# GpSimd's pooling sums of keys and values in pieces of at most 256 columns

## The chip, the cores and the metric

The kernel runs on one core of a Trainium2 chip. The metric is the device time of one execution in microseconds (us). TensorE is called PE in the profile (its weight loads PEld), VectorE is DVE, ScalarE is ACT, GpSimd is POOL, and SyncE, which only issues transfers here, is SP.

## The reference, cut to what matters

Attention with pooled keys and values, then two layers of experts:

```python
k_p = k.reshape(B, H, S // 8, 8, D).mean(axis=3)     # B, H, S, D = 8, 8, 576, 64
v_p = v.reshape(B, H, S // 8, 8, D).mean(axis=3)
scores = q @ k_p.T / sqrt(D);  attn = softmax(scores);  out = attn @ v_p
x = out as (4608, 512)
logits = cosine(x, expert_emb) / tau                 # 8 experts, top 1
x[rows of e] = gate * relu(x @ w1[e]) @ w2[e]        # for each expert e
out = max(x @ m1, x @ m2, x @ m3) @ mo               # (4608, 512)
```

The change concerns the means of eight neighbouring rows of `k` and `v`.

## The kernel before, in words

All of it is one program. The first 200 us are the attention stage: 36 tiles of 128 queries go through a software pipeline (`for it in range(NT + 4)`), in which PE computes scores (`psc`), transposes the weights (`paT`), transposes the next queries (`pqT`) and multiplies by the values (`pav`), in this order in each pass. DVE takes, for each tile, the row maxima (`mx`, L451), the differences (`sh`, L454), the reciprocal sums (`rs`, L500 and L502), the scaled output (`x`, L510) and the routing logits (`dt`, `lg`, L515 and L517). The tiles `psc` and `pav` have one buffer each: PE may overwrite `psc` when `sh` is done, and `pav` when `dt` is done. The two expert layers follow and keep PE busy to the end.

Each of the 8 batches b has its own preparation (`prep_steps`). Its keys lie in the tile `kraw` (`kt` in the code) as 5 chunks of rows, the first four with 128 rows, the last with 64; each row holds 8 neighbours of 64 columns. Its values lie in `vraw` (`vt`) in the same way. The sum over the neighbours is a tree in place, with widths w = 4, 2 and 1: add the upper half to the lower one. `pool_k2` (L262 to L269) does it for the keys of batches 2 to 7, `pool_v` (L275 to L282) for the values of all batches, both on POOL. For batches 0 and 1 DVE sums the keys (L257). After them `spread_v` (L284 to L293), also on POOL, writes the sums into the block layout `vbd` in five instructions. PE transposes the sums (`ptk`, `ptv`). Two generations of `kraw` and `vraw` exist, so the load of batch b + 2 waits on SP's queue until batch b is summed.

The order on every engine is the order of the program. The routing is put between the work of DVE by hand: `fill` takes small steps from a queue and puts them behind the instructions of a tile (`FILL`). Routing works in rounds over groups of tiles (`CHK`). The first round, `rank_steps(0)`, is queued after tile 8, the second, `rank_steps(1)`, after tile 17. A round begins with one scaling of the logits (`lg`, L551), a maximum, a difference (L547), a masked weight (`wt`, L556), a comparison (`oh`, L547), a copy (`pre`, L617) and four adds of a prefix sum (`pre`, L547). Earlier, a few constants are made in the same way (`tokid`, L1422; `im`, L551).

Waits on one engine's own results are semaphore waits too: an instruction that reads what an earlier one of the same engine wrote carries a wait for it, an instruction that reads something else carries none.

Of the kernel before, what the change touches and what calls it, by code (L numbers as in the profile page):

```python
# [14 lines left out]
A = mybir.AluOpType  # L15
# [6 lines left out]
def attention_moe_moe_kernel(  # L22
# [24 lines left out]
    nc = tc.nc  # L47
# [68 lines left out]
    if True:  # L116
# [61 lines left out]
        if True:  # L178
# [69 lines left out]
            def prep_steps(b):  # L248
                kt, vt = kv[b]
                kb, vb = kbds[b % 3], vbds[b % 3]  # L250
                kp = qp.tile([P, 5, 2, D], F32, tag="kp", name=f"kp{b}")
# [11 lines left out]
                def pool_k2():  # L263
                    for c0, c1, n in ((0, 4, P), (4, 5, RC[4])):
                        for w in (4, 2, 1):
                            dst = kt[0:n, c0:c1, 0:w, :] if w > 1 else kp[0:n, c0:c1, 0:1, :]
                            nc.gpsimd.tensor_tensor(
                                dst, kt[0:n, c0:c1, 0:w, :], kt[0:n, c0:c1, w : 2 * w, :], op=A.add
                            )  # L269

                def dup_k():
                    for c0, c1, n in ((0, 3, P), (3, 4, KC[3]), (4, 5, KC[4])):
# [1 line left out]

                def pool_v(c0, c1, n):  # L275
                    for w in (4, 2, 1):
                        for a0 in range(c0, c1, 2) if w == 4 else (c0,):
                            a1 = min(a0 + 2, c1) if w == 4 else c1
                            dst = vt[0:n, a0:a1, 0:w, :] if w > 1 else vp[0:n, a0:a1, :].unsqueeze(2)
                            nc.gpsimd.tensor_tensor(  # L280
                                dst, vt[0:n, a0:a1, 0:w, :], vt[0:n, a0:a1, w : 2 * w, :], op=A.add
                            )  # L282
# [77 lines left out]
                if b == 0:  # L360
                    return [
                        lambda: (pool_all(), dup_k(), trans_k(range(4), 0, 7), trans_k([4], 7, 8)),
                        lambda: (pool_v(0, 4, P), pool_v(4, 5, 64), spread_v()),
                        lambda: (trans_v(0, 4), trans_v(4, 5)),
                        lambda: vdot(),
                    ]
                if b == 1:
                    pk = [lambda c=c: pool_k(c) for c in range(5)]
                    pk += [lambda: (pool_v(0, 4, P), pool_v(4, 5, 64))]
                else:  # L370
                    return [
                        lambda: (pool_k2(), pool_v(0, 4, P), pool_v(4, 5, 64)),
                        spread_v,
                        lambda: trans_kv(range(4), 0),
                        lambda: trans_kv([4], 4 * P),
                        vdot,
                    ]
# [1425 lines left out]
```

## Time and profile before

| what | value |
| --- | --- |
| median of 3 runs | 1263.38 us (1262.02 to 1263.81) |
| the profiled execution's time | 1260.98 us |
| its span on the core | 1259.2 us |
| PE busy | 1215.6 us, 97% of the span |
| DVE busy | 799.2 us, 63% |
| POOL busy | 318.9 us, 25%, in 383 instructions |
| mean granted clock of PE | 0.991 of full speed |

Busy time is the time in which an engine had an instruction running, waits inside an instruction included. The profiled execution is 2.4 us faster than the median of the runs, and its span is 1.8 us shorter than its time.

### The profile page before, as it was taken

To read this page: it belongs to the slowest core of one execution; us is meant where nothing else is said; L and a number is where in the kernel's file an instruction comes from. 1 tells how busy PE (TensorE), PEld (TensorE's weight loads), DVE (VectorE), ACT (ScalarE), POOL (GpSimd) and SP (SyncE) were. 2 spreads that over 40 slices of the span, in tenths; PEclk is the share of its full clock that TensorE was granted. 3 is DMA by queue.
4 is the path that set the end of the run, shared out by engine and by line. 5 is a ranking of instruction groups with operands and counts; after the bars stand their busy time and mean duration, and the time that the engine had idled before them with its cause. 6 is when DMAs were issued, how large, how long until landed. Compare 5 with 4: busy or idle time off the path is not lost. (4 is left out here: it accounts for less than half of the span.)

```text
span 1259.2 us, 22318 instructions
## 1 busy us (share of the span) xinstructions
PE 1215.6 (97%) x8251; PEld 1158.0 (92%) x8251; DVE 799.2 (63%) x1575; ACT 580.5 (46%) x1040; POOL 318.9 (25%) x383
## 2 busy tenths in 40 slices
PE   5899899999999999999999999999999999999995
PEld 4788789999999999999999998998998998998994
DVE  6676886797889999898764446345445454454450
ACT  3466465545666676666655333323223323223221
POOL 6985553420212212222000302103103004004001
PEclk9899999999999999999999999999999999999998
DMA  9968246423976445844619666475564673773721
GB/s 252 267 202 236 97 138 217 151 85 32 298 262 226 164 143 203 283 151 137 207 51 350 241 238 242 160 262 205 207 239 182 220 264 153 258 263 124 253 108 52
DMA packets 98038, 246.21 MB, mean 196 GB/s; under 512 B 17100, under 2 KB 58106, under 8 KB 89858
## 3 DMA queue, kind: packets, MB, share of 16 engines
q1 hardware_dynamic: 84770, 189.09, 44.5%
q0 software_dynamic: 13152, 55.62, 13.3%
q8 instruction: 67, 1.10, 0.4%
q14 instruction: 49, 0.40, 0.1%
HBM read 252.23 MB, written 46.98 MB: 238 GB/s over the span
## 5 line engine op out<-in xcount | busy, mean ns | idle before, releaser
L1617 PE MATMUL p<-yhi,wt 128*128 128x384 f32 x1512 | 387.2, 336 | 0.0
L1617 PEld LDWEIGHTS p<-yhi,wt 128*128 128x128 f32 x1512 | 273.4, 188 | 0.6
L1617 PE MATMUL p<-ylo,wt 128*128 128x384 f32 x756 | 254.0, 336 | 0.0
L1625 ACT COPY s<-p 128x384 f32<-128x384 f32 x162 | 77.8, 480 | 221.1 <-PE p L1617 216.8
L1104 PE MATMUL py<-hhi,whi 128*128 128x256 f32 x576 | 164.6, 286 | 0.0
L1104 PE MATMUL py<-hhi,wlo 128*128 128x256 f32 x576 | 163.1, 283 | 1.6 <-DVE wlo L1036 1.6
L1056 PE MATMUL ph<-xhi,whi 128*128 128x256 f32 x576 | 163.8, 284 | 0.7 <-DVE hlo L1072 0.7
L1056 PE MATMUL ph<-xhi,wlo 128*128 128x256 f32 x576 | 163.0, 283 | 0.7 <-DVE wlo L1036 0.7
L1056 PE MATMUL ph<-xlo,whi 128*128 128x256 f32 x576 | 163.0, 283 | 0.0
L1104 PE MATMUL py<-hlo,whi 128*128 128x256 f32 x576 | 162.9, 283 | 0.0
L1617 PEld LDWEIGHTS p<-ylo,wt 128*128 128x128 f32 x756 | 142.1, 188 | 0.5
L1646 DVE TENSOR_TENSOR blk<-p,s 128x384 f32<-128x384 f32 x108 | 59.7, 553 | 113.9 <-PE p L1617 113.9
L1602 POOL DMA_INDIRECT gt<-gbuf,ix x26 | 37.0, 1424 | 312.1 <-DMA ix<-idbuf 305.7
L1104 PEld LDWEIGHTS py<-hhi,wlo 128*128 128x128 f32 x576 | 110.4, 192 | 1.8 <-DVE wlo L1036 1.8
L1056 PEld LDWEIGHTS ph<-xhi,whi 128*128 128x128 f32 x576 | 110.5, 192 | 1.2 <-DVE hlo L1072 0.9
L1056 PEld LDWEIGHTS ph<-xhi,wlo 128*128 128x128 f32 x576 | 110.5, 192 | 0.9 <-DVE wlo L1036 0.9
L1056 PEld LDWEIGHTS ph<-xlo,whi 128*128 128x128 f32 x576 | 110.5, 192 | 0.0
L1104 PEld LDWEIGHTS py<-hlo,whi 128*128 128x128 f32 x576 | 110.5, 192 | 0.0
L1104 PEld LDWEIGHTS py<-hhi,whi 128*128 128x128 f32 x576 | 110.4, 192 | 0.0
L1036 DVE TENSOR_TENSOR wlo<-w2raw,whi 128x1024 fp32r<-128x1024 f32 x84 | 102.2, 1221 | 8.8 <-ACT whi L1034 8.7
L1036 DVE TENSOR_TENSOR wlo<-w1raw,whi 128x1024 fp32r<-128x1024 f32 x67 | 81.8, 1220 | 27.6 <-ACT whi L1034 26.5
L1034 ACT CAST whi<-w2raw 128x1024 fp32r<-128x1024 f32 x88 | 91.8, 1044 | 7.7 <-PE py L1104 4.7
(316 smaller groups left out, 2280.8 us busy)
## 6 DMA issues: line engine op xcount, KB each, us to landing
wt<-wdram SPq DMA_DIRECT2D x51, 1792.0 KB
w1raw<-in_moe_w_dram SPq DMA_DIRECT2D x88, 512.0 KB
w2raw<-in_moe_w_dram SPq DMA_DIRECT2D x88, 512.0 KB
wdram<-wst POOLq DMA_DIRECT2D x9, 1792.0 KB
ybuf<-yo SPq DMA_DIRECT2D x40, 256.0 KB
cvraw<-in_moe_w_dram POOLq DMA_DIRECT2D x36, 256.0 KB
vraw<-in_v_dram SPq DMA_DIRECT2D x8, 1024.0 KB
xbuf<-x SPq DMA_DIRECT2D x16, 512.0 KB
```

Source lines behind the costliest of these rows:

```text
L1034: nc.scalar.copy(hi, src)
L1036: eng.tensor_tensor(lo, src, hi.bitcast(F32), op=A.subtract)
L1056: nc.tensor.matmul(ps[:, f, :], a_[:, c, fs], b_[:, c, :], start=(n == 0), stop=(n == 3 * DC - 1))
L1104: nc.tensor.matmul(py[:, c // 2, (c % 2) * 256 : (c % 2 + 1) * 256], a_[:, f, c * P : (c + 1) * P], b_[:, f, :], start=(piece == 0 and f = ...
L1602: nc.gpsimd.indirect_dma_start(out=gt[g][:, j : j + 1], out_offset=None, in_=gbuf[:, :], in_offset=bass.IndirectOffsetOnAxis(ap=cols[j], a ...
L1617: nc.tensor.matmul(ps, a_, b_, start=(start and c + n == 0), stop=(c == 1 and n == 2), skip_group_check=True)
L1625: nc.scalar.copy(t, ps)
L1646: tt(src, add[0], add[1], op=A.add)
```

## The change

Each level of the tree is cut into instructions of at most 256 columns: at width w an instruction takes 4 // w chunks. For the keys the level w = 4 (1024 columns) becomes four instructions and the level w = 2 (512 columns) two. For the values the level w = 4 (two instructions of 512 columns) becomes four and the level w = 2 (512 columns) two. The level w = 1 (256 columns) and the chunk of 64 rows stay as they are. The sums and their order are unchanged.

```diff
 def pool_k2():
     for c0, c1, n in ((0, 4, P), (4, 5, RC[4])):
         for w in (4, 2, 1):
-            dst = kt[0:n, c0:c1, 0:w, :] if w > 1 else kp[0:n, c0:c1, 0:1, :]
-            nc.gpsimd.tensor_tensor(
-                dst, kt[0:n, c0:c1, 0:w, :], kt[0:n, c0:c1, w : 2 * w, :], op=A.add
-            )
+            for a0 in range(c0, c1, 4 // w):
+                a1 = min(a0 + 4 // w, c1)
+                dst = kt[0:n, a0:a1, 0:w, :] if w > 1 else kp[0:n, a0:a1, 0:1, :]
+                nc.gpsimd.tensor_tensor(
+                    dst, kt[0:n, a0:a1, 0:w, :], kt[0:n, a0:a1, w : 2 * w, :], op=A.add
+                )
...
 def pool_v(c0, c1, n):
     for w in (4, 2, 1):
-        for a0 in range(c0, c1, 2) if w == 4 else (c0,):
-            a1 = min(a0 + 2, c1) if w == 4 else c1
+        for a0 in range(c0, c1, 4 // w):
+            a1 = min(a0 + 4 // w, c1)
             dst = vt[0:n, a0:a1, 0:w, :] if w > 1 else vp[0:n, a0:a1, :].unsqueeze(2)
```

## Rows read from the trace of the kernel before

**Rows 1.** The page, busy us (share of the span) and instructions of an engine.
```profile
PE 1215.6 (97%) x8251; PEld 1158.0 (92%) x8251; DVE 799.2 (63%) x1575; ACT 580.5 (46%) x1040; POOL 318.9 (25%) x383
```
**Rows 2.** Busy us of each engine in stretches, granted clock of PE, DMA share.
```profile
80.00:93.00 13.00, 10.36 (x87) 9.38 (x86) 12.18 (x28) 7.21 (x20) 11.36 (x13) 1.00 0.44 140
...
125.00:145.00 20.00, 15.17 (x106) 13.15 (x105) 19.16 (x33) 8.75 (x24) 17.40 (x24) 0.91 0.38 133
134.00:136.00 2.00, 2.00 (x9) 1.94 (x9) 2.00 (x4) 0.00 (x0) 1.92 (x3) 0.50 0.02 4
```
**Rows 3.** PE's timeline in the two routing rounds: start, us, work, [idle before].
```profile
91.57 1.22 PE L436 MATMUL psc<-kbd,qT 128*128 128x144 f32 x8 [2.45 <-DVE pre L547]
...
133.77 3.61 PE L490 MATMUL pav<-vbd,aT 128*128 128x146 f32 x12 [3.16 <-DVE dt L515]
142.16 2.07 PE L490 MATMUL pav<-vbd,aT 128*128 128x146 f32 x12 [1.48 <-DVE dt L515]
```
**Rows 4.** DVE's timeline: a constant and steps of the two routing rounds.
```profile
33.76 4.04 DVE L551 TENSOR_SCALAR im<-iof 128x10 f32<-128x10 f32 x1
...
81.36 0.67 DVE L551 TENSOR_SCALAR lg<-lg,rtau 128x72 f32<-128x72 f32 x1
...
85.76 2.75 DVE L617 COPY pre<-oh 128x72 f32<-128x72 f32 x1
...
91.34 0.22 DVE L547 TENSOR_TENSOR pre<-pre 128x72 f32<-128x72 f32 x1
...
129.57 3.92 DVE L547 TENSOR_TENSOR oh<-w,wm 128x72 f32<-128x72 f32 x1
...
137.08 2.62 DVE L547 TENSOR_TENSOR pre<-pre 128x72 f32<-128x72 f32 x1
```
**Rows 5.** POOL's timeline, the pieces beside those steps.
```profile
35.42 3.69 POOL L267 TENSOR_TENSOR kraw<-kraw 128x1024 f32<-128x1024 f32 x2
...
77.58 2.06 POOL L288 TENSOR_TENSOR vbd<-kp,mslot 128x128 f32<-128x128 f32 x5 [1.29 <-PE pav L490]
79.61 3.71 POOL L267 TENSOR_TENSOR kraw<-kraw 128x1024 f32<-128x1024 f32 x2
...
85.98 3.82 POOL L280 TENSOR_TENSOR vraw<-vraw 128x512 f32<-128x512 f32 x3
...
129.06 2.04 POOL L288 TENSOR_TENSOR vbd<-kp,mslot 128x128 f32<-128x128 f32 x5
131.06 3.67 POOL L267 TENSOR_TENSOR kraw<-kraw 128x1024 f32<-128x1024 f32 x2
...
137.10 3.85 POOL L280 TENSOR_TENSOR vraw<-vraw 128x512 f32<-128x512 f32 x3
```
**Rows 6.** POOL by line and shape: busy us, mean ns | idle before.
```profile
L280 POOL TENSOR_TENSOR vraw<-vraw 128x512 f32<-128x512 f32 x24 | 30.1, 1267 | 8.8 <-DMA vraw<-in_v_dram 8.2
...
L267 POOL TENSOR_TENSOR kraw<-kraw 128x1024 f32<-128x1024 f32 x6 | 14.1, 2351 | 0.0
...
L267 POOL TENSOR_TENSOR kp<-kraw 128x256 f32<-128x256 f32 x6 | 4.4, 730 | 0.7 <-PE ptk L313 0.4
```
**Rows 7.** POOL's timeline through the sums of batch 3.
```profile
47.66 3.70 POOL L267 TENSOR_TENSOR kraw<-kraw 128x1024 f32<-128x1024 f32 x2
51.45 0.73 POOL L267 TENSOR_TENSOR kp<-kraw 128x256 f32<-128x256 f32 x1
52.13 1.25 POOL L267 TENSOR_TENSOR kraw<-kraw 64x256 f32<-64x256 f32 x2
...
53.74 3.85 POOL L280 TENSOR_TENSOR vraw<-vraw 128x512 f32<-128x512 f32 x3
57.67 0.72 POOL L280 TENSOR_TENSOR kp<-vraw 128x256 f32<-128x256 f32 x1
```
**Rows 8.** PE's waits in the first 200 us: total us, times, longest us.
```profile
PE pqT L411 <- DMA qgrp<-in_q_dram: 2.9, 1, 2.9
...
PE ptv L336 <- POOL vp L280: 0.7, 1, 0.7
```

## The prediction

> **What bounds the kernel now.** I read the page's busy table first. PE is busy 97% of the span and POOL 25% [rows 1]: time on POOL costs nothing by itself, and a microsecond counts only where PE stands still. So I looked at the granted clock and the busy time by stretch, for places where PE is idle and POOL is pooling, and found two after the start-up: in the 13 us from 80 to 93 PE is busy 10.36, idle 2.64, and in the 20 us from 125 to 145 it is busy 15.17, idle 4.83 [rows 2]. In both DVE is busy nearly throughout, 12.18 and 19.16 us. These are the two routing rounds that fall on pooling. PE's timeline names the waits: a score product waits 2.45 us, two value products 3.16 and 1.48 us, all for DVE [rows 3].
>
> Then I asked DVE's timeline why it is late. A copy of 72 columns takes 2.75 us, a comparison 3.92, an add 2.62, where the same add takes 0.22 when it runs freely [rows 4]. These are not long instructions, they stand still inside. Each ends a few hundredths behind the end of a POOL instruction after which POOL has to wait for its own result: the scaling (81.36 + 0.67 = 82.03) behind the keys' 1024-column sum (79.61 + 2.35 = 81.96), the copy (88.51) behind the second of two 512-column sums (85.98 + 2.49 = 88.47), `im` (37.80) behind 35.42 + 2.35 = 37.77 [rows 4 to 6]. So DVE and POOL exclude each other here, and the price on PE now is 2.64 + 4.83 us of idle time, plus a slower clock after the 3.16 us gap: for 2 us the granted clock is 0.50, the lower of its two levels (1.2 GHz), and the 12 value products take 3.61 us where 12 later take 2.07 [rows 2, 3]: 1.54 us more.
>
> **Where DVE gets in.** This decides the sign. The copy of round one was issued at 85.76 and had the boundary between the two 512-column sums at 87.2 in front of it. These two don't depend on each other, and it did not get in. The add of round two (issued 137.08, ended 139.70) let the same boundary pass at 138.3. The comparison of round two, issued at 129.57, let all that was left of five spreading instructions and the step from them to the keys' sum at 131.06 pass, and ended behind that sum at 133.49; `im` passed 35.42 in the same way [rows 4, 5]. Where POOL has the next independent instruction of 128 rows ready, it starts it about 0.04 us before the last one ends (a 256-column piece takes 0.73, the next instruction starts after 0.68 [rows 6, 7]), and DVE stays out. DVE gets in where POOL waits for its own sum: 47.66 + 2.35 + 1.27 = 51.28, but the third level starts at 51.45, so each of these two gaps is about 0.085 us [rows 6, 7].
>
> The Trainium skill agrees with the overlap: "GPSIMD Engine Reference", section 2.1, says that each of the eight cores goes on to the next instruction when its share of the last is done. It says nothing of when VectorE gets in between.
>
> **The change, part by part.**
> First, POOL's own time. A 256-column piece costs 0.68 us to the start of an independent successor, and 0.73 + 0.085 = 0.81 to that of a dependent one. The levels w = 4 and 2 become six pieces. The first piece of w = 2 needs pieces 1 and 2 of w = 4, the second needs 3 and 4; both were done before or one piece earlier, so I expect no gap until w = 1 needs the sixth: 5 x 0.68 + 0.81 = 4.21 us. Before, it was 51.45 - 47.66 = 3.79 for keys (now +0.42) and 57.67 - 53.74 = 3.93 for values (+0.28) [rows 7]. Six batches of keys and eight of values: 6 x 0.42 + 8 x 0.28 = 4.8 us. The third level and the 64-row chunk stay. The bounds of the gap question are runs of 4.13 us without a gap (six pieces) or of one piece, 0.73; I take the six, by the boundaries above, which have the same kind of instruction and the same 128 rows.
>
> Second, who waits for POOL's sums. Only 0.7 us of PE in the whole stage (the first values), and later PE stands 2.9 us for queries [rows 8], which takes up the 0.28 us of that batch. From then on a sum is used tens of us after it is made. If that cover were gone, up to 4.8 us would show. SP's queue holds the next loads behind the sums; they start at most the same few tenths to 1.1 us later and are used later still. I cost all this at nothing.
>
> Third, DVE's stalls. Before round one POOL has done the values of batch 1 and three batches of both: 0.28 + 3 x 0.70 = 2.38 us late, less the 1.29 us in which it waited for PE at 77.58 [rows 5]: 1.1 us. The keys' run starts at 80.7 instead of 79.61 and has no gap until 80.7 + 4.13 = 84.8. The scaling (81.36) gets out at 84.9 instead of 82.03, so it waits 3.3 us and not 0.45. The copy came 3.73 us after the scaling; now that is 88.6, in the values' run, which goes from 80.7 + 4.21 + 0.68 + 1.61 = 87.2 (1.61 is 53.74 - 52.13 for the 64-row chunk [rows 7]) to 91.3. The copy, or the comparison just ahead of it, waits some 2.8 us there, about as the copy does now (2.53). Round one: 6.1 us of long waits for 3.0, +3.1.
> Round two starts again from DVE (between the rounds POOL waits for slots that DVE computes), so the two stand to each other as before. The spreading is 0.70 later, at 129.76, the keys' run goes from 131.76 to 135.9, and the comparison of 129.57 gets out at 135.97 instead of 133.49: +2.5. The values' run is 137.10 + 0.70 + 0.42 = 138.2 to 142.35. The add that came 3.59 us after the comparison waits 2.6 us, or the add before it, which meets the start of the run, 4.2; now it is 2.4. I take 3.4, +1.0. Sum of the long waits: 3.1 + 2.5 + 1.0 = +6.6 us.
>
> Fourth, what PE feels. Now 3.0 us of long waits cost PE 2.64 us of idle time in round one, and 3.7 + 2.4 = 6.1 cost 4.83 in round two: a share of 0.8 to 0.9. 6.6 x 0.85 = 5.6 us. The clock: PE's gap of 2.45 us left it high, that of 3.16 did not. Round one's gaps grow by about 3 us together, so I add one more slow stretch, 1.5 us (bounds 0 and 3). Sum: +7.1 us. PE has hardly any idle time behind the stage that could take it up [rows 1].
>
> The profiled execution has 1260.98 us, so 1268.1; it is 2.4 us under the median of the runs, which makes 1270.5 for the median. Own range of this case: 1266 (share 0.5, no slow clock) to 1276 (both adds caught, two slow stretches).
>
> **The rivals.**
> *Short pieces let DVE in.* If DVE gets in between any two pieces, nothing waits more than 0.73 us, on average half of it, nine such steps in a round some 3.3 us in small bits, which the slack of each pass (DVE is busy 63% of the span [rows 1]) mostly takes. PE's 2.64 + 4.83 + 1.54 = 9.0 us shrink to 1 or 2: -7.5 us, 1256 for the median. It decides from the point where one boundary of two independent pieces is open. For it: such a wait ends with a POOL instruction each time. Against it: the boundaries at 87.2, 138.3, 131.06 and 35.42 stayed closed. I give it 0.23, for these are few, and none is between 256-column pieces.
> This is also what the Trainium skill would have: "SBUF — State Buffer", section "Who interferes with whom", calls the shared port pair an exclusive lock held for one whole instruction, until whose end the other engine is blocked. By that rule alone shorter instructions mean shorter waits; the trace agrees with the block and its end, not with "one instruction".
> *The gap stays at the level.* If the first piece of w = 2 waits for the fourth of w = 4, the runs are 2.77 and 1.41 us, where they were 2.35 to 2.49 and 1.27. Four long waits grow by about 0.3 us: +1.2, times 0.85 is +1.0, 1264.4: no difference. For it: a wait here is for a count of finished instructions, and the count may be raised once for several pieces. Against it: each pair of chunks has a reader of its own. 0.17.
> *POOL becomes late.* If the sums were needed at once, the 4.8 us of the first part would show: 1268. Against it stand PE's waits [rows 8]. It is inside the case of the forecast, with 0.03 of it.
>
> **How the numbers follow.** Forecast 0.60, open boundaries 0.23, gap at the level 0.17. A difference of 0.2%, 2.5 us, is about what a measurement of this kernel can tell. Slower by more: 0.57 of the first and 0.03 of the third; the same: 0.03 and 0.12; faster: 0.23 and 0.02. The likeliest case gives 1270.5. The range leaves out about 0.07 above and half of the faster case below: 1256 to 1275; the likeliest alone 1266 to 1276.
>
> **What would show it.** In the changed kernel's profile: POOL's timeline with 256-column pieces 0.68 us apart and one gap in six; DVE's scaling of round one and comparison of round two with 3 and 6 us; PE's idle time in the two rounds up from 7.5 to some 13 us, and the lower clock in both. If the long DVE steps are 0.7 us or less, the boundaries are open and I am wrong in the sign; if they end behind the fourth piece, the gap at the level stayed. It would also be wrong if DVE's steps happened to fall beside the runs.

## The result and the profile after

| what | before | after |
| --- | --- | --- |
| median of 20 runs each | 1263.85 us (1260.54 to 1272.40) | 1272.19 us (1268.42 to 1279.90) |
| the profiled execution's time | 1260.98 us | 1270.20 us |
| its span | 1259.2 us | 1267.9 us |

The ratio of the times is 1.0076, with a 95% interval of 1.0060 to 1.0091. The change makes the kernel slower by 0.76%, some 9.6 us (the medians differ by 8.3). The forecast was slower, 1270.5 us.

First the page's busy line of the changed kernel, which answers to [rows 1].

```profile
PE 1218.7 (96%) x8251; PEld 1160.8 (92%) x8251; DVE 808.6 (64%) x1575; ACT 580.3 (46%) x1040; POOL 323.7 (26%) x431
```

POOL has 48 instructions and 4.8 us of work more than before. DVE has the same 1575 instructions and 9.4 us more busy time: the same steps, standing still for longer. POOL's timeline shows what they stand behind (start, us, work; [rows 5] are its counterpart).

```profile
78.01 2.06 POOL L290 TENSOR_TENSOR vbd<-kp,mslot 128x128 f32<-128x128 f32 x5 [0.92 <-PE pav L492]
80.04 4.16 POOL L269 TENSOR_TENSOR kraw<-kraw 128x256 f32<-128x256 f32 x6
...
86.57 4.13 POOL L282 TENSOR_TENSOR vraw<-vraw 128x256 f32<-128x256 f32 x6
90.78 0.72 POOL L282 TENSOR_TENSOR kp<-vraw 128x256 f32<-128x256 f32 x1
91.46 1.24 POOL L282 TENSOR_TENSOR vraw<-vraw 64x256 f32<-64x256 f32 x2
...
134.45 4.12 POOL L269 TENSOR_TENSOR kraw<-kraw 128x256 f32<-128x256 f32 x6
...
140.92 4.13 POOL L282 TENSOR_TENSOR vraw<-vraw 128x256 f32<-128x256 f32 x6
```

And DVE's timeline of the changed kernel, for [rows 4]:

```profile
33.13 4.93 DVE L553 TENSOR_SCALAR thq<-iof 128x13 f32<-128x13 f32 x1
...
81.80 2.46 DVE L553 TENSOR_SCALAR lg<-lg,rtau 128x72 f32<-128x72 f32 x1
...
87.08 3.71 DVE L549 TENSOR_TENSOR oh<-w,wm 128x72 f32<-128x72 f32 x1
90.85 0.70 DVE L619 COPY pre<-oh 128x72 f32<-128x72 f32 x1
...
128.36 1.77 DVE L553 TENSOR_SCALAR lg<-lg,rtau 128x72 f32<-128x72 f32 x1
...
132.95 5.71 DVE L549 TENSOR_TENSOR oh<-w,wm 128x72 f32<-128x72 f32 x1
...
140.73 4.42 DVE L549 TENSOR_TENSOR pre<-pre 128x72 f32<-128x72 f32 x1
...
170.20 0.43 DVE L553 TENSOR_SCALAR lg<-lg,rtau 128x48 f32<-128x48 f32 x1
```

Lay the two beside each other. Six pieces run for 4.12 to 4.16 us, and each long step ends a few hundredths behind the last of six: the scaling at 84.26 (the run ends at 84.20), the comparison of round one at 90.79 (90.70), that of round two at 138.66 (138.57), the add at 145.15 (145.05). The scaling had three boundaries between pieces in front of it, the other three steps five each: 18 boundaries, and DVE got in at none. (The scaling of round two, issued at 128.36, ends in the same way, at 130.13 behind a run of the values that ends at 130.07.) What follows each run is the instruction into `kp`, which needs the run's last sum: POOL starts it 0.08 us after the run's end (84.28, 90.78), and DVE is through.

What PE makes of it stands in PE's timeline (idle time before in brackets, for [rows 3]) and in the busy time by stretch, for [rows 2].

```profile
38.78 0.74 PE L424 MATMUL psc<-kbd,qT 128*64 128x144 f32 x2 [3.67 <-DVE sh L456]
...
91.07 2.07 PE L492 MATMUL pav<-vbd,aT 128*128 128x146 f32 x12 [3.48 <-DVE dt L517]
92.98 1.22 PE L347 MATMUL pd<-enT,vT 64*128 64x16 f32 x10
94.14 1.25 PE L438 MATMUL psc<-kbd,qT 128*128 128x144 f32 x8
95.22 0.71 PE L469 MATMUL paT<-ident,at 128*128 128x128 f32 x5
95.77 0.60 PE L413 MATMUL pqT<-ident,qgrp 128*128 128x128 f32 x4
...
138.94 3.83 PE L492 MATMUL pav<-vbd,aT 128*128 128x146 f32 x12 [5.47 <-DVE dt L517]
142.57 2.13 PE L347 MATMUL pd<-enT,vT 64*128 64x16 f32 x10
145.96 2.26 PE L438 MATMUL psc<-kbd,qT 128*128 128x144 f32 x8 [1.25 <-DVE pre L549]
148.01 1.27 PE L469 MATMUL paT<-ident,at 128*128 128x128 f32 x5
149.07 1.06 PE L413 MATMUL pqT<-ident,qgrp 128*128 128x128 f32 x4
149.93 2.34 PE L492 MATMUL pav<-vbd,aT 128*128 128x146 f32 x11
```
```profile
80.00:97.00 17.00, 12.41 (x101) 11.26 (x101) 16.76 (x32) 8.58 (x23) 12.62 (x21) 1.00 0.47 157
128.00:152.00 24.00, 16.86 (x94) 14.99 (x92) 21.54 (x29) 8.85 (x24) 18.75 (x33) 0.72 0.28 98
139.00:150.80 11.80, 10.55 (x43) 9.77 (x44) 10.57 (x17) 2.61 (x7) 8.06 (x14) 0.50 0.11 44
```

PE's idle time in the two rounds is 17.00 - 12.41 = 4.59 and 24.00 - 16.86 = 7.14 us, 11.73 where it was 7.47: +4.3. Then the clock. In round one it stays at 1.00 after a gap of 3.48 us; in round two, after 5.47 us, it is 0.50 (1.2 GHz), and every group from 138.94 to 149.93 takes nearly twice what the same work takes from 91.07 on: 3.83 for 2.07, 2.13 for 1.22, 2.26 for 1.25, 1.27 for 0.71, 1.06 for 0.60, and eleven products 2.34 for 11/12 of 2.07. That is 5.1 us, where before lost 1.54: +3.6. Together +7.9 us.

The same is seen from the starts of the three rounds. Those of before, from DVE's timeline (the first is in [rows 4]):

```profile
125.76 0.98 DVE L551 TENSOR_SCALAR lg<-lg,rtau 128x72 f32<-128x72 f32 x1
...
162.05 0.78 DVE L551 TENSOR_SCALAR lg<-lg,rtau 128x48 f32<-128x48 f32 x1
```

Rounds one, two and three start at 81.36, 125.76 and 162.05 before, at 81.80, 128.36 and 170.20 after: 0.4, 2.6 and 8.2 us later. So the start-up gives 0.4, round one 2.2, round two 5.5 us, and the span as a whole is 8.7 us longer: the expert layers behind give nothing back.

### The profile page after: what moved, and what is told of

It reads as the page before. It is cut to its first block, busy times and chain, and to the rows that moved or that the text cites. A ratio compares the mean times of both kernels' runs of the same rounds, so it can differ in the third digit from the quotient of the medians.

```text
span 1267.9 us, 22366 instructions
## 1 busy us (share of the span) xinstructions
PE 1218.7 (96%) x8251; PEld 1160.8 (92%) x8251; DVE 808.6 (64%) x1575; ACT 580.3 (46%) x1040; POOL 323.7 (26%) x431
## 5 line engine op out<-in xcount | busy, mean ns | idle before, releaser
L1038 DVE TENSOR_TENSOR wlo<-w1raw,whi 128x1024 fp32r<-128x1024 f32 x67 | 81.8, 1220 | 25.7 <-ACT whi L1036 24.5
```

The costliest lines, as they stand in the source:

```text
L1038: eng.tensor_tensor(lo, src, hi.bitcast(F32), op=A.subtract)
```

## The experiments

The theory tested: DVE gets in only where POOL's next instruction waits for the result of the one before; a run of independent instructions shuts it out to its end, however short they are. Rivals: the loss is POOL's 4.8 us of later sums (lateness); the number of instructions, not their order, does it; the loss has to do with one of the two trees alone. Each kernel is before with one edit, unless it says otherwise; ratios are to before, in five rounds, with 95% intervals.

**One tree at a time.** The first kernel has the keys' half of the diff alone, the second the values' half.

> Only the keys' sums are cut into pieces; the values' stay as before. Theory of the runs (VectorE stays out between independent pieces of 128 rows and gets in where GpSimd waits for its own sum): the scaling of round one now ends behind six pieces, some 2 us later than before, and the comparison of round two takes 5.7 us instead of 3.9, while the add of round two that meets the values' sums stays near 2.6. TensorE loses 3 to 6 us, so the kernel is 3 to 6 us over the one before. Rival, GpSimd's own lateness (48 more instructions, 4.8 us): keys have 2.5 of the 4.8 us, so half of the change's loss, some 4 us, but with no reason for one step of VectorE to grow rather than another.

> Only the values' sums are cut into pieces; the keys' stay as before. Theory of the runs: in round one the step that meets the values' sums of batch 5 waits up to 4.1 us instead of 2.75, in round two the scaling 1.8 instead of 1.0 and the add that meets batch 7's values 4.4 instead of 2.6; the comparison of round two stays at 3.9. TensorE loses 2 to 5 us. Rival, lateness: values have 2.2 of the 4.8 us, some 4 us.

Keys alone 1.0033 (1.0017 to 1.0049), values alone 1.0031 (1.0016 to 1.0046); the two add up to 0.64% of the 0.76%. Each half lengthens the steps beside its own run: with the keys cut, a scaling at 77.07 takes 5.86 us and the comparison of round two 5.69, while its add stays at 2.77 (2.62 before); with the values cut, the add takes 4.25 us and the comparison stays at 3.91 (3.92 before). Neither tree alone is the cause. The times alone, some 4 us for each half, are also what lateness would give; it is the steps that tell the two apart. One size was missed: the scaling was to come out some 2 us later, and takes 5.2 us longer, since here it fell at the beginning of the spreading. With the values cut, the scaling of round two takes 1.25 us where 1.8 were expected.

**The same pieces in another order.** Both kernels have the change's pieces, as many and as long. The one interleaves the levels, so that POOL has to wait for itself after two pieces; the other puts the piece that w = 2 needs first to the end of w = 4, so that it waits after four.

```diff
+def pieces(c0, c1):
+    if c1 - c0 == 1:
+        return [(4, c0, c1), (2, c0, c1), (1, c0, c1)]
+    return [(4, 0, 1), (4, 1, 2), (2, 0, 2), (4, 2, 3), (4, 3, 4), (2, 2, 4), (1, 0, 4)]
...
+    # the other order:
+    return [(4, 1, 2), (4, 2, 3), (4, 3, 4), (4, 0, 1), (2, 0, 2), (2, 2, 4), (1, 0, 4)]
```

> The same instructions as the change, 256 columns each and as many, in another order: two pieces of the first level, the piece of the second level that needs them, the other two, their second level, the third level. So GpSimd waits for its own sum three times in seven pieces and not once. Theory of the runs: the longest run is 2.1 us instead of 4.1, VectorE's long steps fall to 2.1 us or less (but for the comparison behind the spreading), and the loss is gone: between 5 us under and 2 us over the kernel before. Rival, lateness or the number of instructions: both are as in the change, so some 8 us over the kernel before.

> The same instructions as the change with one piece moved: the first chunk's piece of the first level comes last of its level, so that the second level has to wait for it. The run of six pieces becomes one of four (2.8 us) and one of two (1.4 us), nearly the 2.35 to 2.5 and 1.27 us of the kernel before. Theory of the runs: VectorE's long steps are those of the kernel before plus 0.3 to 0.4 us, the time within 3 us of the kernel before (0 to +3). Rival, lateness or the number of instructions: some 8 us over, as the change.

With a wait after two pieces the ratio is 0.9985 (0.9969 to 1.0001): the change's whole loss is gone, with its instructions all there. Its two longest steps, 3.50 us each, lie behind the spreading and two pieces, as DVE's and POOL's timelines show for round one; no other step of the rounds takes over 0.78.

```profile
80.01 3.50 DVE L550 TENSOR_TENSOR oh<-w,wm 128x72 f32<-128x72 f32 x1
```
```profile
80.02 2.04 POOL L291 TENSOR_TENSOR vbd<-kp,mslot 128x128 f32<-128x128 f32 x5
82.03 4.36 POOL L272 TENSOR_TENSOR kraw<-kraw 128x256 f32<-128x256 f32 x6
```

The step ends at 83.51; the second piece ends at 82.03 + 0.68 + 0.73 = 83.44. The five spreading instructions, independent too, had shut it out before.

With a wait after four pieces the ratio is 1.0034 (1.0015 to 1.0053), 4.3 us where 0 to 3 were expected. DVE's timeline shows why the size was missed:

```profile
79.04 4.96 DVE L559 SCALAR_TENSOR_TENSOR wt<-lg,w 128x72 f32<-128x72 f32 x1
...
131.76 4.86 DVE L550 TENSOR_TENSOR oh<-w,wm 128x72 f32<-128x72 f32 x1
```

I had counted the runs of pieces and not what stands ahead of them. Spreading (2.04 us) and four pieces (81.15 to 83.92) are one closed stretch, which the step of 79.04 leaves at 84.00, and here a step of each round fell at its beginning; before, one did. The end points are those of the theory.

**Lateness alone.** Before, with one instruction on POOL behind the keys and one behind the values of each batch, which makes everything behind it later (0.41 us each, 14 of them: 5.7 us in all) without lengthening a run of sums. The idle instruction does stand without a wait ahead of the values' run and of the spreading, and so makes those stretches 0.4 us longer.

```diff
+idle = ap1.tile([P, 384], F32, name="idle")
...
+nc.gpsimd.memset(idle, 0.0)
```

> The kernel before with one more GpSimd instruction behind each batch's keys and each batch's values, a fill of 384 columns of a tile that nothing reads, by the fills of the kernel before (1.06 us for 1152 columns) about 0.4 us each: 14 of them make GpSimd some 5 us slower in the stage, as the change does, with no run of sums cut into pieces. Theory of the runs: VectorE's long steps stay near those of the kernel before, the time within 2.5 us of it. Rival, lateness: some 8 us over the kernel before.

1.0020 (1.0002 to 1.0038), 2.6 us by the medians, where the theory allowed 2.5, with more delay on POOL than the change makes. Lateness as the main cause would have given some 8. What part of the 2.6 us is lateness can't be told from the longer stretches and a shift of the steps against the runs: the comparison of round two takes 4.28 us here (3.92 before), the copy of round one 3.12 (2.75), the add 2.71 (2.62).

**A chain in place of a tree.** The four full chunks are summed in seven adds of 256 columns into one target, each of which needs the one before; the order of the additions is changed, nothing is left out.

```diff
+for j in range(1, 8):
+    src = kt[0:P, 0:4, 0:1, :] if j == 1 else kp[0:P, 0:4, 0:1, :]
+    nc.gpsimd.tensor_tensor(kp[0:P, 0:4, 0:1, :], src, kt[0:P, 0:4, j : j + 1, :], op=A.add)
```

> The four full chunks are summed in a chain, not in a tree: seven instructions of 256 columns, each of which adds one more neighbour to the running sum and so waits for the one before it. The order of the additions is another one. Theory of the runs: each boundary of the sums is open, the long steps beside the sums fall to 0.8 us; only behind the five spreading instructions a step can still wait 2.8 us. TensorE's gaps in the two rounds nearly go, 3 to 8 us under the kernel before. GpSimd works some 1.2 us longer on each group of sums, 17 us in all. Rival, lateness or the number of instructions: more of both than in the change, so over 8 us slower than the kernel before.

0.9948 (0.9928 to 0.9968): the same instructions of 256 columns, as many and as long as the change's, and faster than before by 0.5%. All steps of the rounds take 0.78 us or less, but for those beside the spreading, which the edit left closed. One such step on DVE's timeline, and POOL's beside it:

```profile
122.76 2.99 DVE L624 COPY pre<-oh 128x72 f32<-128x72 f32 x1
```
```profile
122.97 2.05 POOL L295 TENSOR_TENSOR vbd<-kp,mslot 128x128 f32<-128x128 f32 x5
124.97 0.72 POOL L266 TENSOR_TENSOR kp<-kraw 128x256 f32<-128x256 f32 x1
125.77 4.75 POOL L266 TENSOR_TENSOR kp<-kp,kraw 128x256 f32<-128x256 f32 x6
```

The copy ends at 125.75, behind the first add of the chain (125.69), after which POOL waits for itself.

**One opening, and its control.** Before, with a copy of one column on POOL behind the spreading. In the one kernel it reads what the last spreading instruction wrote; in the control it reads a constant, so that POOL waits for nothing.

```diff
+seen = ap1.tile([P, 1], F32, name="seen")
...
+nc.gpsimd.tensor_copy(seen[0:64], vb[0:64, SL[4], 0:1])
...
+# the control:
+nc.gpsimd.tensor_copy(seen[0:64], mslot[0:64, SL[4], 0:1])
```

> The kernel before with one small GpSimd copy behind the five spreading instructions of each batch, which reads one column that the last of them wrote, so that GpSimd has to wait once before it goes on to the keys' sums. Theory of the runs: the comparison of round two (3.9 us before) gets in there and takes under 2 us; the steps that meet only the sums stay; 0 to 3 us under the kernel before. If boundaries are not what lets VectorE in, the comparison stays at 3.9 us and the time at that of the kernel before or 0.5 us over it.

> The control of the copy behind the spreading: the same small copy at the same place in the kernel before, but it reads a constant and so waits for nothing. Theory of the runs: a step that is caught by the spreading passes the copy too and waits for the end of the keys' first sum, as in the kernel before (3.9 us); the time is that of the kernel before, within 2.5 us. If the small copy itself, or its 64 rows, lets VectorE in, the result is that of the copy that waits, some 5 us under the kernel before.

0.9957 (0.9937 to 0.9977) with the dependence, 0.9997 (0.9980 to 1.0015) without. DVE's and POOL's timelines in round two, first of the kernel with the dependence, then of the control:

```profile
129.99 1.37 DVE L549 TENSOR_TENSOR oh<-w,wm 128x72 f32<-128x72 f32 x1
```
```profile
131.24 0.28 POOL L289 TENSOR_TENSOR vbd<-kp,mslot 64x64 f32<-64x64 f32 x1
...
131.59 0.18 POOL L295 COPY seen<-vbd 64x1 f32<-64x1 f32 x1
```
```profile
129.71 4.04 DVE L549 TENSOR_TENSOR oh<-w,wm 128x72 f32<-128x72 f32 x1
```
```profile
131.19 0.18 POOL L295 COPY seen<-mslot 64x1 f32<-64x1 f32 x1
131.33 3.68 POOL L268 TENSOR_TENSOR kraw<-kraw 128x1024 f32<-128x1024 f32 x2
```

The comparison, issued at the same place of the spreading (0.51 us behind its start in both), comes out at 131.36 in the one, and at 133.75 behind the keys' 1024-column sum in the other. One instruction of 0.18 us, in the same place and as long: the dependence makes the difference. It does so one boundary earlier than the theory says. The wait lies behind the fifth spreading instruction, which runs from 131.24 to 131.52 on 64 rows; at 131.36 the comparison was already out, 0.09 us behind the fourth (131.27). The gain was 0 to 3 us by expectation and came out at 5.4 by the ratio, 3.3 by the medians. The kernel's runs lie wide apart (1255 to 1267 us, the profiled one 1266.72), so this profile doesn't show where the rest came from.

**Openings in the change itself.** The changed kernel, with such a dependent copy behind four of the six pieces.

```diff
 nc.gpsimd.tensor_tensor(
     dst, kt[0:n, a0:a1, 0:w, :], kt[0:n, a0:a1, w : 2 * w, :], op=A.add
 )
+if c1 == 4 and w > 1 and a1 < c1:
+    nc.gpsimd.tensor_copy(seen[0:n], kt[0:n, a0, 0, 0:1])
...
# and the same for the values, with vt
```

> The changed kernel itself, with one small GpSimd copy behind four of the six pieces of the first two levels, which reads one column that the piece has just written, so that GpSimd waits there; the pieces and their order are those of the change. The longest run of sums is then two pieces, 1.4 us, and not six. Theory of the runs: VectorE's long steps beside the sums fall to 1.5 us, only a step behind the spreading can wait some 2.8 us; the loss of the change is gone and the time is 3 to 8 us under the kernel before, near that of the chain. Rival, that short instructions or their number are what costs: still some 8 us over the kernel before, and more by the copies (56 of them).

0.9915 (0.9886 to 0.9945), where the change without the copies has 1.0076: 1.6% between the two, by instructions that do nothing. That is 7.8 us under before by the medians, 10.7 by the ratio, against 3 to 8 expected. POOL is busy for 334.4 us, more than in the change. The comparison's 3.71 and 5.71 us are gone; DVE's and POOL's timelines show the only long step left in round one, again behind the spreading and one piece, out at the first copy:

```profile
81.40 0.72 DVE L554 TENSOR_TENSOR oh<-w,wm 128x72 f32<-128x72 f32 x1
...
83.92 2.48 DVE L554 TENSOR_TENSOR pre<-pre 128x72 f32<-128x72 f32 x1
```
```profile
83.59 2.04 POOL L295 TENSOR_TENSOR vbd<-kp,mslot 128x128 f32<-128x128 f32 x5
85.59 0.71 POOL L270 TENSOR_TENSOR kraw<-kraw 128x256 f32<-128x256 f32 x1
86.37 0.18 POOL L274 COPY seen<-kraw 128x1 f32<-128x1 f32 x1
```

**A version that beats both.** The chain, and dependent copies behind three of the spreading instructions (`if c in (1, 3, 4)`).

> The chain of seven dependent adds and three small copies in the spreading (behind its second, fourth and fifth instruction), each of which waits for what was just written. Theory of the runs: no step of VectorE beside GpSimd takes over 1.1 us, TensorE has no gap over 1 us in the two rounds, 5 to 9 us under the kernel before. Rival, lateness or the number of instructions: slower than the chain alone and than the change.

0.9861 (0.9835 to 0.9888), 1247.48 us, 16 us under before, against 5 to 9 us expected. The busy time of the stretches that hold rounds one and two, and DVE's starts of rounds one and three:

```profile
75.00:97.00 22.00, 21.62 (x167) 19.01 (x166) 16.93 (x46) 13.86 (x37) 20.16 (x36) 1.00 0.78 236
117.00:140.00 23.00, 22.80 (x176) 19.95 (x174) 18.04 (x47) 14.18 (x37) 20.93 (x38) 1.00 0.39 138
```
```profile
75.54 0.50 DVE L561 TENSOR_SCALAR lg<-lg,rtau 128x72 f32<-128x72 f32 x1
...
147.53 0.50 DVE L561 TENSOR_SCALAR lg<-lg,rtau 128x48 f32<-128x48 f32 x1
```

PE stands still for 0.38 and 0.20 us and its clock is 1.00 in both. From round one to round three it takes 71.99 us where before takes 80.69: 8.7 less, the 6.9 us of idle time and 1.54 of slow clock that before had there, nearly all. Another 5.8 us lie ahead of round one, which starts at 75.54 instead of 81.36; the expectation had not counted the start-up. (The two profiled spans differ by 13.7 us, so 0.8 are lost again behind.)

**What sets the closed boundaries apart.** The theory is too wide as it stands. In the start-up of the changed kernel a run of six pieces begins behind a wait of 0.95 us for its load, and DVE gets in behind its first piece, as POOL's and DVE's timelines show:

```profile
25.32 0.74 POOL L282 TENSOR_TENSOR vraw<-vraw 128x256 f32<-128x256 f32 x1 [0.95 <-DMA vraw<-in_v_dram]
```
```profile
25.51 0.60 DVE L549 TENSOR_TENSOR tokid<-tokid,cc 128x36 f32<-128x36 f32 x1
```

The piece ends at 26.06 and POOL had started the next, independent one at 26.02; the step is out at 26.11. The next such step, issued at 26.15, gets out at 26.83 behind the second piece (26.78) in the same way. These are the pieces of the change, as long and on as many rows. What differs is what lies ahead of the run: the runs with the 18 boundaries follow, without a wait between, an instruction on 64 rows (the fifth of the spreading, or the last sum of the 64-row chunk).

The attention stages of the twelve traces bear this out. At every wait of POOL that a stalled step met, DVE got in. At a boundary without a wait it got in each time (some 40) if POOL had run only 128-row instructions since its last wait. Behind a 64-row instruction of the same stretch it stayed out at every boundary between two 128-row ones (some 170); what opened there led into a 64-row instruction with a wait close behind it, as at 131.27 above. So the dependence works by the wait that it makes, and pieces without a dependence shut DVE out where the run follows a 64-row instruction without a wait. This is read from the traces; no run moved a 64-row instruction alone.

## Why the prediction was right

**Where DVE gets in** carried the sign, and held for the runs that the forecast was about: the 18 boundaries of the changed kernel, the order of the pieces (0.9985 with a wait after two, 1.0076 after six), and the copy with and without a dependence show it. The rule behind it was too wide. The four boundaries that it was read from (87.2, 138.3, 131.06 and 35.42) all lie behind a 64-row instruction without a wait between, and so do the 18; the prediction didn't name this condition, and that it was met again was luck. The 0.68 us was read at a boundary of the other kind, from the third level to the 64-row chunk: in the changed kernel the copy of 90.85 ends at 91.55, behind such a third-level sum (to 91.50), although POOL had started the next instruction at 91.46.

**POOL's own time** was +4.8 us and is +4.8; six pieces to the start of what needs them were 4.21 us and are 4.24, 4.21 and 4.19. That it costs nothing by itself was not quite shown: 5.7 us of delay on POOL gave 2.6 us, of which some is the longer stretches and the shift against the runs.

**The long waits** were +3.1 and +3.5 us. Taken as durations over the 0.22 us of a free step, they are 2.24 + 3.49 = 5.73 in round one (+2.8) and 5.49 + 4.20 = 9.69 in round two (+3.6). In round one the parts differ: the keys' run starts at 80.04, 0.4 us late and not 1.1, since POOL still waits 0.92 us for PE ahead of it; the scaling waits less than I had (2.24 for 3.3), the comparison more (3.49 for 2.8). In round two the add took the upper of its two bounds (4.20), and the scaling, which the forecast left out, takes 1.77 us for 0.98.

**Two terms were mis-sized and made up for each other.** That the sum came out this near is luck. The share of the waits that PE feels was 0.85; it is 4.3 of 6.35 us, 0.67, which gives 4.3 for 5.6. The clock was 1.5 us, for a slow stretch in round one; it is 3.6, all of it in round two. I had read from two gaps (2.45 us harmless, 3.16 not) that a longer gap of round one would bring the lower clock. The gap there grew to 3.48 and it stayed at 1.00, while the gap of 5.47 us in round two was followed by some 12 us of work at the lower clock (138.94 to 150.8). Before had some 3.4 us of it and not 2: the 2 us are the length of the stretch that [rows 2] show, and the lower clock went on to 137.4.

```profile
136.00:137.40 1.40, 1.40 (x7) 0.87 (x5) 1.40 (x4) 0.20 (x1) 1.24 (x4) 0.50 0.00 0
```

The 1.54 us that it cost hold, for they are read from the twelve products. Sum 7.9 for 7.1.

**The start-up** was to cost nothing, covered by PE's wait for queries. It gave 0.4 us, but not in that way: a DVE step of 4.93 us at 33.13 now makes PE wait 3.67 us for `sh`, and the 2.9 us in which PE waited for queries are gone.

**The rivals.** Short pieces that let DVE in would have given 1256; the trace shows steps of 2.5 to 5.7 us behind pieces of 0.73. In the run that begins behind a wait (25.32) DVE did get in behind single pieces, as that rival has it for all. The rule of the Trainium skill that stood with it ("SBUF — State Buffer", section "Who interferes with whom": the lock lasts for one whole instruction, the other engine is blocked until its end) agrees with the trace on the block, and on its end only where the run begins behind a wait. The gap at the level did not stay: the pieces of w = 2 follow those of w = 4 without a wait (six in 4.13 us). Lateness is answered by the run with the idle instruction.

**What stays open.** Why the clock fell where it did was not isolated. The start-up was not taken apart either: round one starts between 73.6 and 81.8 us in these kernels, so a given step meets another part of a run, and effects on single steps are read with that in mind. Why a 64-row instruction keeps the boundaries behind it closed until POOL waits is not shown either, and whether a wait right behind it would open the change's runs of six was not tried.

## What to carry to other kernels

Where two engines exclude each other, the length that counts can be that of a whole stretch without a wait, and not that of the instruction: look in the timeline for what a stalled step ends behind, and count from there back to the last place where the other engine had to wait for itself. Look also at what the stretch begins with: here the closed ones held an instruction on fewer rows. Cutting a long instruction into independent pieces made such a stretch worse (longer in sum, and gaps that stood between levels closed); putting dependent instructions next to each other, or a tiny dependent one in between, opened it. An engine that is busy for 25% of the span can cost the busiest engine its time through a third one, and the place to find it is the stretch, not the page's sum.

## What the runs showed of the hardware

- A wait for its own result on POOL, some 0.08 us, is enough for DVE to get in; an independent copy (0.18 us) did not let it in: the comparison took 1.37 us beside a copy that waits and 4.04 beside one that doesn't.
- Without a wait, DVE got in between independent 128-row pieces where POOL had run only 128-row instructions since its last wait (26.06 and 26.78 in the changed kernel), and at none of 18 such boundaries behind a 64-row instruction.
- Such a stretch of POOL instructions shuts DVE out across changes of operation too: five spreading multiplications and four sums, 4.96 us for one step.
- The granted clock of TensorE stayed at 1.00 after a gap of 3.48 us and was 0.50 after gaps of 3.16 (in before) and 5.47 us; the work behind the longest ran at 0.50 for some 12 us, that in before for 3.4.
